# Issuing the first weight load of a decode kernel as 16 partitions and then 112 partitions

## The chip, the cores and the metric

The kernel runs on one core of a Trainium2 chip. The metric is the device time of one execution in microseconds (us), the median of several runs. Beside it stand the profile of one execution (a page of summaries, and views of the trace) and, in the same trace, one record for each packet that the DMA engines moved: its queue, start, length in time and bytes. In the views, PE is the engine of the matrix products, DVE, ACT and POOL are the engines that work on vectors, and SP (SyncE) issues DMAs. The span of a profile is one to two us shorter than the run's time.

## The reference, cut to what matters

One decode step for two tokens. Attention with 16 query heads and 8 key/value heads over a cache of 32,768 positions, a small dense layer beside it, and a gate that mixes the two:

```python
q = (x @ wq)                       # x 2 x 448, wq 448 x 4096
scores = einsum("bhqd,bhkd->bhqk", q, k) * (Dh ** -0.5)
o = einsum("bhqk,bhkd->bhqd", softmax(scores), v)
a = o @ wo
b = gelu(x @ w1 + b1) @ w2 + b2
return g * a + (1 - g) * b
```

The K and V caches are 512 MiB, everything else together about 10 MB. Each byte is read once, so the time is the time to read it (547.43 MB at the 430 GB/s of before's page are 1273 us).

## The kernel before

SBUF holds a ring of three slots of 64 KB per partition. SyncE (SP) issues all large loads in a fixed order: wq and the dense weights share slot 0, then K and V tiles of 8 MB rotate through the slots.

```python
order = [("WQ", 0), ("W12", 0)]
for i in range(NTILES + LAG):
    if i < NTILES: order.append(("K", i))
    if i >= LAG and i - LAG < LASTV: order.append(("V", i - LAG))
# ... cut ...
for d in order:                                   # SP's program
    for pd in before_of[d]:
        E.wait("pe", released(pd))                # the slot is free
    kind, idx = d
    if kind == "WQ":
        parts = [(wq_f, A_wq[0:KC * P, :].rearrange("(p k) n -> p (k n)", p=P), "d_wq0"),
                 (wq_r, A_wq[KC * P:Dm, :].rearrange("p (h n) -> (p h) n", h=2), "d_wq1")]
        for i, (o, src, _) in enumerate(parts):
            dma(lambda e, o=o, src=src: e.dma_start(o, src), "slot0", ("wq", i))
    # ... W12, WO and the last V cut ...
    else:
        src = kv_src(A_k_cache if kind == "K" else A_v_cache, idx)
        dma(lambda e, src=src, d=d: e.dma_start(cut(slot_of[d], 0, SLOT), src),
            f"slot{slot_of[d]}", ("fill", d))
# ... cut: PE's program begins with the products on wq
E.wait("slot0", ("wq", 1))                        # all of wq has landed
```

`wq_f` has 128 partitions (P = 128) with rows of 3 x 4096 bf16 values, 24,576 bytes, one packet each.

## Time and profile before

| | before |
|---|---|
| time, median | 1274.05 us (1273.9 to 1274.08, 3 runs) |
| span of the profile | 1272.2 us |
| DMA | 9 tenths or more in 39 of 40 slices, 430 GB/s |
| PE, DVE busy | 55%, 54% |
| first packet of the large queue, last large packet | 1.765 us, 1268.105 us |

The page of before, slices of the span (each digit or number is one fortieth of it), and the line of the large queue (packets, megabytes, share of the 16 engines' time):

```profile
DMA  9999999999999999999999999999999999999998
GB/s 409 429 433 429 437 441 427 433 427 441 431 437 435 429 431 433 439 431 437 435 429 431 439 433 431 439 433 429 431 441 431 435 437 431 431 433 439 431 423 353
...
q1 hardware_dynamic: 10804, 547.43, 99.6%
```

The DMA engines never run dry between the first slice and the last. The packet records say it more sharply: from the first packet of this queue (1.765 us) to the last large one (1268.105 us), about 16 packets are in flight. The page's chain of waits names DVE and PE for 34% of the span, but while they work to free one slot, the loads of the others keep the engines full.

The start of before: the timeline of SP's issues (start, duration), the page's line of PE's products on wq (busy, mean ns, idle before), and the page's lines of the two wq loads (KB, us from issue to landing):

```profile
0.74 0.88 SPq L370 DMA_DIRECT2D ring<-in_A_wq_dram  x2
1.67 1.83 SPq L376 DMA_DIRECT2D ring<-in_B_w_dram  x3
3.54 0.98 SPq L391 DMA_DIRECT2D ring<-in_A_k_cache_dram  x2
...
L419 PE MATMUL ps_s<-xT,ring 128*128 128x2 bf16 x128 | 3.6, 165 | 8.2 <-DMA ring<-in_A_wq_dram 8.2
...
ring<-in_A_wq_dram SPq DMA_DIRECT2D x1, 3072.0 KB, 10.6
ring<-in_A_wq_dram SPq DMA_DIRECT2D x1, 512.0 KB, 11.4
```

SP is far ahead of the engines: K's first load is issued at 3.54 us and its first packets start at 18.56 us.

The same start by windows (busy time of each engine, the granted clock, the share of the DMA engines, GB/s):

```profile
2.00:10.00 8.00, 0.27 (x5) 0.21 (x5) 2.48 (x11) 1.45 (x2) 1.88 (x5) 1.00 0.87 357
10.00:18.00 8.00, 4.97 (x165) 4.42 (x165) 1.85 (x7) 1.33 (x3) 0.00 (x0) 1.00 1.04 432
...
100.00:1200.00 1100.00, 597.62 (x3768) 114.37 (x1461) 597.04 (x436) 34.86 (x154) 0.00 (x0) 0.78 1.00 433
```

A packet is counted where it starts, so short windows swing a little; the full rate of this kernel is the 433 GB/s of the last line.

### The profile page before, as it was taken

What the parts mean: (1) busy time and instruction counts of PE and PEld (TensorE: products, weight loads), DVE (VectorE), ACT (ScalarE), POOL (GpSimd) and SP (SyncE); (2) the same over time, 40 slices, a digit from 0 to 9 for tenths busy, and PEclk for the clock granted to TensorE, in tenths of its full rate; (3) what the DMA queues carried; (4) which work ended last, traced back from release to release, by engine and by line L of the source; (5) the groups of instructions that cost most, each with busy time, mean ns of one, the idle gap of its engine ahead of it and who ended that gap; (6) DMA issues with size and microseconds to landing.
All of it is one profiled execution on the core that took longest, in us unless ns stands there. A gap on an engine that the chain in (4) does not pass through costs nothing.

```text
span 1272.2 us, 8282 instructions
## 1 busy us (share of the span) xinstructions
PE 693.5 (55%) x4640; PEld 145.3 (11%) x2112; DVE 686.0 (54%) x529; ACT 43.8 (3%) x184; POOL 3.3 (0%) x14
## 2 busy tenths in 40 slices
PE   4566566545566444765445655445664546654465
PEld 3111111100111000111001111001110001110011
DVE  2675546745376553655635567353665536556351
ACT  1000000000000000000000000000000000000000
POOL 1000000000000000000000000000000000000000
PEclk9978887777887677877778877788877788867786
DMA  9999999999999999999999999999999999999998
GB/s 409 429 433 429 437 441 427 433 427 441 431 437 435 429 431 433 439 431 437 435 429 431 439 433 431 439 433 429 431 441 431 435 437 431 431 433 439 431 423 353
DMA packets 10973, 547.62 MB, mean 430 GB/s; under 512 B 1352, under 2 KB 1616, under 8 KB 1872
## 3 DMA queue, kind: packets, MB, share of 16 engines
q1 hardware_dynamic: 10804, 547.43, 99.6%
q8 instruction: 9, 0.15, 0.0%
q14 instruction: 4, 0.03, 0.0%
q10 hardware_dynamic: 156, 0.01, 0.0%
HBM read 547.43 MB, written 0.00 MB: 430 GB/s over the span
## 4 chain that ended last, share of the span: by engine, by line
DMA 63%; DVE 20%; PE 14%; issue 3%; SPq 0%; another core or an unknown queue 0%; DVEq 0%
DMA ring<-in_A_k_cache_dram 60%; DVE ring L720 18%; PE ps_s L487 4%; PE ps_s L334 4%; PE ps_o L334 3%; DMA ring<-in_A_v_cache_dram 3%; DVE mx L724 1%; PE ps_o L536 1%; PE ps_m L496 0%; PE ps_m L501 0%; DVE gmax L726 0%; PE ps_f L548 0%; DVE gmx L730 0%; SPq L376 0%
## 5 line engine op out<-in xcount | busy, mean ns | idle before, releaser
L720 DVE STREAM_TRANSPOSE ring<-ring 128x2048 uint32<-128x2048 uint32 x256 | 565.2, 2274 | 393.0 <-DMA ring<-in_A_k_cache_dram 392.8
L487 PE MATMUL ps_s<-ring,Abd 128*128 128x512 bf16 x1024 | 426.1, 416 | 429.8 <-DVE ring L720 429.4
L334 PE MATMUL ps_s<-ring,Abd 128*128 128x512 bf16 x1024 | 422.8, 413 | 0.0
L487 PEld LDWEIGHTS ps_s<-ring,Abd 128*128 128x128 bf16 x1024 | 106.0, 104 | 851.5 <-DVE ring L720 483.5
L334 PE MATMUL ps_o<-ring,PT 128*24 128x512 bf16 x1504 | 111.9, 404 | 0.0
L536 PE MATMUL ps_o<-ring,PT 128*24 128x512 bf16 x544 | 57.1, 418 | 12.8 <-DMA ring<-in_A_v_cache_dram 12.8
L506 PE MATMUL ps_f<-o_sb,selg 128*32 128x257 f32 x32 | 17.0, 636 | 83.4 <-DVE o_sb L761 83.4
L761 DVE SCALAR_TENSOR_TENSOR o_sb<-ps_o,mask,o_sb 128x256 f32<-128x256 f32 x112 | 54.2, 484 | 9.1 <-PE ps_o L536 5.1
L724 DVE TENSOR_REDUCE mx<-ps_s 128x1 f32<-128x1024 f32 x16 | 19.6, 1225 | 60.0 <-PE ps_s L334 60.0
L632 ACT ACTIVATE negm<-ps_m 128x1 f32<-128x1 f32 x16 | 2.7, 171 | 1157.6 <-PE ps_m L501 1157.6
L737 DVE STREAM_TRANSPOSE PT<-pexp 128x1024 bf16<-128x1024 bf16 x16 | 19.9, 1244 | 36.8 <-PE ps_o L334 36.8
L536 PEld LDWEIGHTS ps_o<-ring,PT 128*24 128x24 bf16 x544 | 14.6, 98 | 102.3 <-issue 85.3
L734 DVE COPY ls<-lsum 128x1 f32<-128x1 f32 x16 | 2.5, 154 | 31.8 <-ACT pexp L636 31.8
L626 ACT COPY Abd<-qrep 32x16 bf16 (+1 forms) x128 | 19.4, 199 | 0.6
L636 ACT ACTIVATE pexp<-ps_s,negm 128x1024 bf16<-128x1024 f32 x16 | 17.8, 1113 | 1.7
L496 PE MATMUL ps_m<-ident_f,mx 128*1 128x128 f32 x32 | 6.1, 270 | 21.1 <-DVE mx L724 21.1
L758 DVE TENSOR_SCALAR o_sb<-ps_o,mask 128x256 f32<-128x256 f32 x16 | 7.6, 475 | 15.7 <-PE ps_o L334 15.7
L506 PEld LDWEIGHTS ps_f<-o_sb,selg 128*32 128x32 f32 x32 | 2.9, 141 | 101.5 <-DVE o_sb L761 101.5
L501 PE MATMUL ps_m<-ones_f,gmx 1*128 1x1 f32 x32 | 6.0, 256 | 9.9 <-DVE gmx L730 9.9
L726 DVE TENSOR_REDUCE gmax<-ps_m 1x2 f32<-1x128 f32 x16 | 4.5, 278 | 7.5 <-PE ps_m L496 7.5
L419 PE MATMUL ps_s<-xT,ring 128*128 128x2 bf16 x128 | 3.6, 165 | 8.2 <-DMA ring<-in_A_wq_dram 8.2
L501 PEld LDWEIGHTS ps_m<-ones_f,gmx 1*128 1x128 f32 x32 | 4.7, 183 | 14.6 <-DVE gmx L730 14.6
(76 smaller groups left out, 61.5 us busy)
## 6 DMA issues: line engine op xcount, KB each, us to landing
ring<-in_A_v_cache_dram SPq DMA_DIRECT2D x1, 4096.0 KB, 26.8
ring<-in_A_v_cache_dram SPq DMA_DIRECT2D x2, 2048.0 KB, 33.5
ring<-in_A_wq_dram SPq DMA_DIRECT2D x1, 3072.0 KB, 10.6
ring<-in_B_w_dram SPq DMA_DIRECT2D x1, 1568.0 KB, 17.9
ring<-in_A_wo_dram SPq DMA_DIRECT2D x1, 1568.0 KB, 32.4
ring<-in_B_w_dram SPq DMA_DIRECT2D x1, 1344.0 KB, 13.7
ring<-in_A_wo_dram SPq DMA_DIRECT2D x1, 1344.0 KB, 35.3
ring<-in_A_wq_dram SPq DMA_DIRECT2D x1, 512.0 KB, 11.4
```

The costliest lines, as they stand in the source:

```text
L334: return e.add_instruction(mybir.InstMatmult(name=f"I-{nc.next_id()}", engine=mybir.EngineType.PE, ldweights=False, ins=[e.lower_ap(x), e. ...
L487: fn = lambda e, o=o, x=x, st=st, sp=sp, s=s, w=w: e.matmul(o, a_win(s, w), x, start=st, stop=sp, skip_group_check=True)
L501: E.ins(lambda e: e.matmul(ps_m[:, C_BC:C_BC + 1], gmx[:, :], ones_f[0:1, 0:1], start=True, stop=True), key=("M2", g))
L506: E.ins(lambda e: e.matmul(ps_oa, selg[:, :], o_sb[:, :], start=False, stop=False, skip_group_check=True), key=("OT", g))
L536: fn = lambda e, o=o, x=x, wt=wt, st=st, sp=sp, j=j: e.matmul(o, wt, x, start=st, stop=sp, skip_group_check=True)
L626: E.ins(lambda e, o=o, Q=Q, c=c: e.copy(o[:, :, c:c + 2], qrep[32 * Q:32 * Q + 32, :, bass.ds(E.dyn(2 * g, 2), 2)]), key=(("A", g) if (Q = ...
L636: E.ins(lambda e: e.activation(pexp[:, :].rearrange("p (r i a) -> p i r a", r=CR, i=2), ps_s[:, :].rearrange("p (i r a) -> p i r a", i=2, ...
L720: E.ins(lambda e: e.transpose(k_words(idx, blk), k_words(idx, blk)), key=("T", idx, blk))
L724: E.ins(lambda e: e.tensor_reduce(mx[:, :], ps_s[:, :], AX.X, ALU.max), key=("MX", g))
L737: E.ins(lambda e: e.transpose(PT[:, :], pexp[:, :]), key=("PT", g))
L758: E.ins(lambda e, p=p, m=m: e.tensor_scalar(o_sb[:, 0:Dh], p, m, None, op0=ALU.mult), key=("OS0", g))
L761: E.ins(lambda e, p=p, m=m: e.scalar_tensor_tensor(out=o_sb[:, 0:Dh], in0=p, scalar=m, in1=o_sb[:, 0:Dh], op0=ALU.mult, op1=ALU.add), key= ...
```

## The change

The likely intent is an earlier first byte: a first DMA with few rows might be ready sooner, with the other 112 rows right behind it. All else stays, and PE still waits for all of wq.

```diff
                 if kind == "WQ":
-                    parts = [(wq_f, A_wq[0:KC * P, :].rearrange("(p k) n -> p (k n)", p=P), "d_wq0"),
-                             (wq_r, A_wq[KC * P:Dm, :].rearrange("p (h n) -> (p h) n", h=2), "d_wq1")]
-                    for i, (o, src, _) in enumerate(parts):
+                    src = A_wq[0:KC * P, :].rearrange("(p k) n -> p (k n)", p=P)
+                    parts = [(wq_f[0:16, :], src[0:16, :]), (wq_f[16:P, :], src[16:P, :]),
+                             (wq_r, A_wq[KC * P:Dm, :].rearrange("p (h n) -> (p h) n", h=2))]
+                    for i, (o, src) in enumerate(parts):
                         dma(lambda e, o=o, src=src: e.dma_start(o, src), "slot0", ("wq", i))
...
-                E.wait("slot0", ("wq", 1))
+                E.wait("slot0", ("wq", 2))
```

## The prediction

> **What bounds the kernel.** Its DMA stream, from almost the first microsecond to the last four. The slices show DMA 9 tenths in 39 of 40, 430 GB/s over the span. The packet records of the big queue (q1) show 16 packets in flight from its first packet, at 1.74 us, to 1268.1 us of a span of 1272.2 us. Compute sits inside that: PE 55%, DVE 54%. The chain of waits names DVE and PE for 34%, but while they free a slot, the loads of other slots keep the queue full. So a microsecond won or lost by the stream at the start should come out, nearly whole, at the end.
>
> **What changes.** The same 3072 KB of wq move in two DMAs (16 rows of 24,576 B, one for each of 16 engines; then 112 rows, seven each) instead of one of 128 (eight each). PE still waits for all of wq.
>
> 1. *One more issue on SP:* 0.41 us (timeline, 0.74 to 1.15). Cost 0: the first packets last until 3.3 us or later, the second DMA is issued by about 1.6 us, and K's first load, issued at 3.54, moves data only at 18.5 us.
> 2. *Perhaps an earlier first byte* (the likely intent). Issue begins at 0.74, first packet at 1.74, the engines start over 0.33 us. I take −0.15 us.
> 3. *Where the rows land.* [...] a packet of 24,576 B takes 0.912 us. [...] Some hides behind the cold start, since the first packets take 1.4 to 2.5 us already: I take +2.2.
> 4. *The 112 rows.* [...] +1.8 us, ±0.5 for unevenness.
>
> No trace of before has a large load on fewer than 128 partitions[...].
>
> **On the critical path:** all of 2, 3 and 4, since the stream has no slack. Sum: −0.15 + 2.2 + 1.8 = about +3.9 us, to 1278.0 us (+0.3%). [...] Range 1273.6 to 1281.5. Faster by over 2% 0.003, within 2% 0.99, slower by over 2% 0.007: even wq at a quarter rate throughout costs about 22 us, under 2%.
>
> **What would show it.** The first 16 packets of q1: right if they take about 3 to 3.7 us, wrong if 1.4 to 2.5. The 112 rows: packets of up to twice 0.912 us. PE's first product on wq (now 12.73 us) and K's first packets (18.54 us) some 3 to 5 us later; steady packets of 65,536 B still 2.42 us; the last packet later by the same; idle times of PE and DVE moved, not grown.
>
> **What would make it wrong.** [...] rows dealt in strides of 16 instead of blocks of seven[...]; engines that fall behind at the start without setting the end; a first byte that gains more than 0.3 us.

The forecast's sum came to −0.15 + 2.2 + 1.8, about +3.9 us, so 1278.0 us. The +2.2 us for the 16 rows (2.7 us for longer packets, less 0.5 for what hides behind the slow first ones) and the +1.8 us for the 112 rows: both were assumed, and no trace of before showed them.

(The prediction's 1.74 and 18.54 us for the first packets of the queue and of K are the 1.765 and 18.56 us of the packet records above.)

## More of the kernel before

The experiments ran in several sets on different chips; the median of before was 1274.03 to 1274.14 us in each set of repeated runs.

The end of before (timeline), which will matter later; the output is issued by SP once ACT and DVE have written it:

```profile
1269.03 0.50 ACT L653 CAST pexp<-ps_f 2x112 bf16<-2x112 f32 x2 [41.61 <-PE ps_f L548]
1269.03 0.54 DVE L792 CAST pexp<-ps_f 2x112 bf16<-2x112 f32 x2 [3.27 <-PE ps_f L548]
1269.96 0.34 SPq L395 DMA_DIRECT2D out_dram<-pexp  x1
```

## The result, and the profile after

The time after is 1279.09 us (1278.34 to 1279.26, 4 runs), before 1274.07 us (4 runs): 5.0 us more. The ratio is 1.0038, 95% interval 1.0021 to 1.0056, so slower, by far less than 2%. (A ratio here is the mean time of one kernel's fast runs over that of the other's of the same rounds, so not quite the ratio of the medians that are quoted.) It was inside the predicted range (1273.6 to 1281.5), with 1278.0 as the forecast.

The page of after, slices and queue:

```profile
DMA  9999999999999999999999999999999999999998
GB/s 315 452 429 426 435 427 442 431 427 437 431 441 429 427 439 431 441 429 427 439 431 441 429 427 439 431 441 429 427 439 433 439 429 427 439 433 439 429 422 368
...
q1 hardware_dynamic: 10820, 547.43, 99.7%
```

The engines are as "busy" as before, with the same bytes, but the first slice moved 315 GB/s in place of 409. So the busy share does not tell the rate: in the windows from 2 to 10 us below and above, shares of 0.86 and 0.87 stand beside 200 and 357 GB/s. The start of after, the same three views (the last line is from the list of all DMA issues, since the page leaves it out):

```profile
0.74 1.38 SPq L371 DMA_DIRECT2D ring<-in_A_wq_dram  x3
2.15 1.46 SPq L377 DMA_DIRECT2D ring<-in_B_w_dram  x3
3.66 0.91 SPq L392 DMA_DIRECT2D ring<-in_A_k_cache_dram  x2
...
L420 PE MATMUL ps_s<-xT,ring 128*128 128x2 bf16 x128 | 3.6, 165 | 14.1 <-DMA ring<-in_A_wq_dram 14.1
...
ring<-in_A_wq_dram SPq DMA_DIRECT2D x1, 2688.0 KB, 16.0
...
ring<-in_A_wq_dram SPq DMA_DIRECT2D x1, 512.0 KB, 16.8
...
ring<-in_A_wq_dram SPq DMA_DIRECT2D x1, 384.0 KB, 5.5
```

The further issue on SP cost nothing: K's first load is issued 0.12 us later, some 20 us before it is due. PE's wait for wq grew from 8.2 to 14.1 us. By windows:

```profile
2.00:10.00 8.00, 0.27 (x5) 0.21 (x5) 2.08 (x10) 1.45 (x2) 1.88 (x5) 1.00 0.86 200
10.00:18.00 8.00, 0.00 (x0) 0.00 (x0) 1.98 (x7) 0.20 (x1) 0.00 (x0) 1.00 0.92 257
...
100.00:1200.00 1100.00, 613.27 (x3791) 116.81 (x1472) 603.20 (x439) 34.90 (x154) 0.00 (x0) 0.77 1.00 433
```

The loss is all in the first 18 us: 200 and 257 GB/s in place of 357 and 432. From 100 us on the rate is 433 in both. The packet records of the 128 rows of `wq_f`, taken sixteen at a time in order of start (so, one packet for each engine, although the records do not name the engine):

```
              before                         after
round   median start  median length    median start  median length   rows of
  0        1.88           1.74            1.86           2.55        the DMA of 16
  1        3.59           0.94            4.42           2.20        the DMA of 112
  2        4.52           0.92            6.62           1.65
  3        5.45           0.91            8.26           1.40
  4        6.37           0.91            9.67           1.29
  5        7.28           0.91           10.98           1.36
  6        8.20           0.91           12.35           1.64
  7        9.11           0.91           13.99           1.51
K's first 18.85           2.42           24.91           2.42
```

The first packet started at 1.755 us against 1.765: nothing was gained there. The median length was longer in all eight rounds, and from round 1 on the shortest packet of after (1.25 us) was longer than the longest of before (0.97 us). K's first packets started 6.1 us later (24.91 less 18.85), and the last large packet of the kernel ended 6.1 us later (1274.20 less 1268.11). Yet the span grew by only 5.1 us. From the last large packet to the end of the span there are 4.08 us before and 3.05 us after. So there is a loss of 6.1 us at the start, and a gain of 1.0 us at the end that nobody had asked for. Here is the end of after; the output's issue follows the writes by less than in before:

```profile
1275.11 0.50 ACT L654 CAST pexp<-ps_f 2x112 bf16<-2x112 f32 x2 [41.82 <-PE ps_f L549]
1275.11 0.54 DVE L793 CAST pexp<-ps_f 2x112 bf16<-2x112 f32 x2 [3.27 <-PE ps_f L549]
1275.71 0.32 SPq L396 DMA_DIRECT2D out_dram<-pexp  x1
```

### The profile page after: what moved, and what is told of

It is laid out like the page before. It is cut to its first block, busy times and chain, and to the rows that moved or that the text cites. A ratio compares the mean times of both kernels' runs of the same rounds, so it can differ in the third digit from the quotient of the medians.

```text
span 1277.3 us, 8288 instructions
## 1 busy us (share of the span) xinstructions
PE 700.7 (55%) x4640; PEld 146.1 (11%) x2112; DVE 685.9 (54%) x529; ACT 43.9 (3%) x184; POOL 3.3 (0%) x14
## 4 chain that ended last, share of the span: by engine, by line
DMA 63%; DVE 18%; PE 16%; issue 3%; SPq 0%; another core or an unknown queue 0%; DVEq 0%
DMA ring<-in_A_k_cache_dram 60%; DVE ring L721 16%; PE ps_s L488 5%; PE ps_s L334 5%; PE ps_o L334 4%; DMA ring<-in_A_v_cache_dram 3%; PE ps_o L537 1%; DVE mx L725 1%; PE ps_m L502 0%; PE ps_m L497 0%; DVE gmax L727 0%; PE ps_f L549 0%; DVE gmx L731 0%; SPq L377 0%
## 5 line engine op out<-in xcount | busy, mean ns | idle before, releaser
L334 PE MATMUL ps_o<-ring,PT 128*24 128x512 bf16 x1504 | 115.8, 416 | 0.0
L537 PE MATMUL ps_o<-ring,PT 128*24 128x512 bf16 x544 | 58.4, 428 | 12.7 <-DMA ring<-in_A_v_cache_dram 12.7
L420 PE MATMUL ps_s<-xT,ring 128*128 128x2 bf16 x128 | 3.6, 165 | 14.1 <-DMA ring<-in_A_wq_dram 14.1
```

The lines of the kernel that those rows point to most:

```text
L334: return e.add_instruction(mybir.InstMatmult(name=f"I-{nc.next_id()}", engine=mybir.EngineType.PE, ldweights=False, ins=[e.lower_ap(x), e. ...
L537: fn = lambda e, o=o, x=x, wt=wt, st=st, sp=sp, j=j: e.matmul(o, wt, x, start=st, stop=sp, skip_group_check=True)
```

## The experiments

The theory: the partitions that the DMA engines write at the same time set the length of the packets, and 16 neighbouring partitions at a time make them longer than the single load of all 128 does. The texts call this the ports theory, after the picture of what lies behind it. No run shows that picture. The packets of 3.65 and of about 1.8 us in the expectations were assumed; measured were 3.17 to 3.29 (blocks16) and 1.75 to 1.92 us (stride8, half64). Rival A: an additional DMA, or a small one, costs the time by itself. Rival C: the small first DMA spoils the cold start, in which packets are slow anyway (a median of 1.74 us in round 0 of before, 0.91 to 0.94 in the later rounds). Later rivals concern the HBM side, and how rows are dealt to engines. The record marks all runs as correct, and that includes blocks16_src8, whose edit permutes rows of wq: so the check does not notice a wrong wq, and its mark says little about the edits. The diffs show the deciding lines only: the load of `wq_r` is kept in all, and PE always waits for the whole of wq.

### cols: the same two sizes, cut by columns

```diff
+ parts = [(wq_f[:, a:b], src[:, a:b]) for a, b in ((0, 1536), (1536, KC * HD))]
```

> wq's first load in two DMAs as in the change, but cut by columns: 128 rows of 3,072 B, then 128 rows of 21,504 B. The byte split is the change's (1/8, 7/8), the count of DMAs is the change's, and every DMA has all 128 partitions. Ports theory: no loss, 1274.1 us within 0.5, K's first packets at 18.6 us. Rival A (a further DMA in the queue, or a small first one, costs the time): about 1279 us, as the change.

1272.97 us (1272.8 to 1273.86) against 1274.03 of before, ratio 0.9993 (0.9976 to 1.0010). The bytes of both DMAs are those of the change, and nothing is lost. PE's wait for wq, from the page of cols:

```profile
L420 PE MATMUL ps_s<-xT,ring 128*128 128x2 bf16 x128 | 3.5, 165 | 7.9 <-DMA ring<-in_A_wq_dram 7.9
```

Rival A falls. The median is even 1 us below before; that was not expected, and is taken up under k0_cols. Since cols has as many DMAs as the change, it is the fairer kernel to compare the change with: 1279.09 less 1272.97 is 6.1 us, the loss that the packets show.

### blocks16, stride8, half64: which partitions are written together

```diff
+ parts = [(wq_f[16 * j:16 * j + 16, :], src[16 * j:16 * j + 16, :]) for j in range(8)]   # blocks16
+ parts = [(wq_f[j:P:8, :], src[j:P:8, :]) for j in range(8)]                             # stride8
+ parts = [(wq_f[a:a + 64, :], src[a:a + 64, :]) for a in (0, 64)]                        # half64
```

> The same load as eight DMAs of 16 neighbouring partitions. Ports theory: [...] packets of 24,576 B take 2.5 us (what the first 16 of the change took) to 3.65 us[...], and the load 20 to 29 us in place of 7.3: 1286 to 1296 us. Rival A (a cost per DMA, 5 us for one more): 35 us more, 1309 us. Rival C (only the cold start suffers): 1279 us or less, packets after the first 16 at 0.91 us.

> Eight DMAs of 16 partitions as in blocks16, but each takes every eighth partition[...]. Ports theory: packets of 24,576 B about 1.8 us, the load some 14.6 us in place of 7.3: about 1281 us, a third of the loss of blocks16. Rivals A and C: the same as blocks16, since number, size and row count of the DMAs are the same.

> Two DMAs of 64 partitions, 0 to 63 and 64 to 127, four rows for each engine. Ports theory with rows dealt in blocks (as I take it for the 112 rows): [...] packets 1.8 us, the load 14.6 us: about 1281 us. Rows dealt in strides of 16: [...] packets 2.5 to 3.65 us, 1286 to 1296 us. Rival A: 1279 us. Rival C: 1279 us or less, packets of the second half 0.91 us.

| | partitions of one DMA | time, us | packets of rounds 1 to 7, medians, us | over cols, us | K's first packets (median) later than in cols, us |
|---|---|---|---|---|---|
| blocks16 | 16 neighbouring | 1291.33 | 3.17 to 3.29 | 18.4 | 18.0 |
| stride8 | 16, 8 apart | 1280.42 | 1.75 to 1.90 | 7.5 | 7.5 |
| half64 | 64 neighbouring | 1280.92 | 1.79 to 1.92 | 8.0 | 7.8 |
| before | all 128 | 1274.03 | 0.91 to 0.94 | | |

(The times over cols are differences of the medians.) PE's wait for wq, from the pages of blocks16, stride8 and half64:

```profile
L420 PE MATMUL ps_s<-xT,ring 128*128 128x2 bf16 x128 | 3.6, 165 | 25.8 <-DMA ring<-in_A_wq_dram 25.8
```
```profile
L420 PE MATMUL ps_s<-xT,ring 128*128 128x2 bf16 x128 | 3.6, 165 | 15.5 <-DMA ring<-in_A_wq_dram 15.5
```
```profile
L420 PE MATMUL ps_s<-xT,ring 128*128 128x2 bf16 x128 | 3.6, 165 | 15.7 <-DMA ring<-in_A_wq_dram 15.7
```

blocks16 and stride8 issue the same number of DMAs, of the same size and row count; only which partitions stand together differs, and the loss is 18.4 against 7.5 us. The choice of partitions makes the difference, and both times are as expected for it (1286 to 1296 us, and about 1281); rivals A and C had the same loss for both, and C fails too because late packets are as slow as early ones (3.17 to 3.29 us in rounds 1 to 7). A round of 16 packets of 24,576 bytes in 3.2 us is 123 GB/s, in 1.75 to 1.92 us 205 to 225; the window from 10 to 20 us shows 121 GB/s in blocks16, that from 5 to 10 us 222 in stride8 and 212 in half64. (In stride8 and half64 the first packet also came 0.3 to 0.4 us later, at 2.13 and 2.08 us against 1.76 in cols, which is a small part of their loss.) half64 also tells something of how rows are dealt to engines. Dealt in strides of 16, each of its rounds would write 16 neighbouring partitions, as blocks16 does, whose packets took 3.17 to 3.29 us; they took 1.79 to 1.92. That fits a deal in blocks of four neighbouring rows. How the single load of 128 rows is dealt, no run tells. And delays at the start reach the end whole: the last two columns agree within 0.4 us.

### blocks16_src8: SBUF's side or HBM's

```diff
+ parts = [(wq_f[16 * j:16 * j + 16, :], src[j:P:8, :]) for j in range(8)]
```

> Wrong result on purpose (rows of wq permuted): the partitions of blocks16, fed from the rows of HBM that stride8 reads together. If the SBUF side limits (ports): blocks16's time, 1291.3 us. If the HBM side does (which rows are read together): stride8's, 1280.4 us.

1290.99 us; packets of rounds 1 to 7 have medians of 3.16 to 3.30 us. It is blocks16's time. The time follows the partitions that are written (blocks16, 1291.33 us), not the rows of HBM that are read (stride8, 1280.42 us).

### swap: the 112 rows first

```diff
+ parts = [(wq_f[0:112, :], src[0:112, :]), (wq_f[112:P, :], src[112:P, :])]
```

> 112 rows (0 to 111) first, then the 16 rows 112 to 127. Ports theory: the same sum in another order, the 16 rows [...] 3.2 us a packet: 1278 to 1280 us. Rival C (a small first DMA spoils the cold start): with 112 rows first the loss goes, 1273 to 1274 us.

1279.58 us (1279.35 to 1279.61). The loss does not need a small DMA at the start: rival C falls. Here the last 16 packets of the load took 2.0 to 3.2 us.

### k0_16_112: the same cut on K's first load

```diff
+ rows = (0, 16, P) if d == ("K", 0) else (0, P)
+ for a, b in zip(rows, rows[1:]):
+     dma(... cut(slot_of[d], 0, SLOT)[a:b, :], src[a:b, :] ...)
```

> wq as before; the first load of K (rows of 65,536 B, running after 18 us) in 16 and 112 partitions. Ports theory: the loss scales with bytes, 6.1 us x 65,536 / 24,576 = 16.3 us over a kernel with the same number of DMAs and no loss (1273.0): about 1289 us; packets of the 16 rows 3.2 x 2.67 = 8.5 us in place of 2.42. Rival C: no loss, 1273 to 1274 us. Rival A: 1279 us.

1295.75 us (1294.4 to 1296.69), 22.8 us over cols. Rivals A and C fall again, but the size is a miss: 16.3 us were expected. The packets say where the other 6.5 us are. The 16 rows took a median of 8.65 us, as expected, 6.2 more than the 2.42 of a full load; but in the change the first round cost only 0.85 us, presumably because part of the added time hid behind the cold start (no run isolates this), and scaled by 2.67 that is 2.3. This is 3.9 us of the miss. The seven rounds of the 112 rows had a mean of 4.46 us (of the medians), where the change's, 1.58 us, scales to 4.21: seven times 0.25 is 1.8. And the first packets of the next K load, which meet the last of the 112 rows, took 3.2 us in place of 2.42: 0.8. So the cut is dearer in the middle of a stream than at its cold start, by more than its bytes.

### stride7: how the 112 rows are dealt

```diff
+ parts = [(wq_f[0:16, :], src[0:16, :])] + [(wq_f[16 + j:P:7, :], src[16 + j:P:7, :]) for j in range(7)]
```

> The change's first DMA of 16 rows, then the other 112 rows as seven DMAs of 16 rows, 7 partitions apart (16, 23, 30 ...; then 17, 24, 31 ...). If the single DMA of 112 rows deals blocks of seven neighbouring rows, these are the very sets of partitions that its rounds write: the change's time again, 1279.1 us within 0.7, and packets of the same lengths (medians 2.2, 1.65, 1.4, 1.3, 1.35, 1.6, 1.5 us). If the 112 rows are dealt otherwise: another time. [...]

1278.89 us, and medians of 2.17, 1.67, 1.44, 1.26, 1.33, 1.63 and 1.58 us for the seven rounds, within 0.07 us of the change's in each. So the single DMA of 112 rows behaves as one that deals blocks of seven neighbouring rows, whose rounds write partitions 7 apart. No packet of any round is near 0.91 us: the shortest of all 112 took 1.16 us. This is where the prediction's picture broke: it let only a few packets of a round be slow, by an estimate whose working is cut. Why the rounds differ among themselves, from 1.26 to 2.17 us, no run tells.

### four_same and four_apart: whose packets become longer

One run each. An extra small DMA of four rows, into partitions 0 to 3 in four_same and 0, 4, 8 and 12 in four_apart, runs just ahead of K's first load; K's load then uses all 128 partitions as always. The question is whether the small DMA slows only the few engines that it concerns (the "sharers" of the text) or the others too. (SP also waits for the small DMA before K's third load; the diff leaves this out.)

```diff
+ xo = cut(0, W_WQ + W_W12, FREE)[0:4:1, :]     # four_same; [0:16:4] in four_apart
+ xi = kv_src(A_k_cache, 0)[0:4:1, 0:FREE]
+ dma(lambda e: e.dma_start(xo, xi), "d_ex", "ex")
```

> before with one extra small DMA ahead of K's first load, into memory that is free then: 4 rows of 11,776 B into partitions 0 to 3, so 4 of the 16 engines[...]. Both theories: the four extra packets about 4 x 0.437 = 1.7 us (11,776 / 24,576 of 0.912 us is 0.437). Only the sharers suffer (as predicted): of K's first 48 packets of 65,536 B, [...] at most a few[...] differ. All suffer: most of K's first 16 packets[...] are longer than 2.5 us.

> The control of four_same: the same four rows into partitions 0, 4, 8 and 12[...]. Extra packets 0.44 us each, K's packets all 2.42 us.

Packet lengths in us:

```
              the four extra packets     K's first 16 packets
four_same     0.44 0.47 0.80 1.49        13 of 3.01 to 3.25, and 2.88, 2.62, 2.47
four_apart    0.44 0.45 0.45 0.45        15 of 2.42 to 2.43, and 2.88
```

(The next 48 packets of both are 2.42 to 2.43 us.) The bytes are the same, the rows of HBM differ a little, and at most four of the 16 engines have an extra packet (taking one packet in flight for each engine, as in before's records, where about 16 are in flight). With the four partitions apart nothing happens (a single packet of 2.88 us stands in both); with the four neighbouring ones, 13 of the first 16 packets of K's load became 0.6 to 0.8 us longer, and at least nine of these ran on engines that had no extra packet. So here four packets to neighbouring partitions held up engines that had no part in them. Why, no run here tells.

### k0_cols and wait_sp: the microsecond at the end

```diff
+ cols = (0, SLOT // 8, SLOT) if d == ("K", 0) else (0, SLOT)     # k0_cols: two DMAs by columns
+ if d == ("K", 0): E.wait("pool", "ts1")                         # wait_sp: one wait more on SP
```

> wq as before, in one DMA; the first load of K in two DMAs of 128 partitions, cut by columns (1/8, 7/8). It asks why cols is 1.06 us faster than before. Tail theory: [...] the fetch of two 8 KB blocks that stands before the output's packets at 1270.6 us of before lies elsewhere: 1273.0 us, and no such fetch between the output's issue and its packets. Rival (cols gains because wq's first packets are short): 1274.0 us, as before.

> before with one more wait in SyncE's program, on a memset-like instruction done at 4.0 us, ahead of K's first load: no transfer is changed. Tail theory, if a few instructions are enough to move the fetch: 1273.0 us; if they are not: 1274.0 us, and the fetch still there. No theory expects more than 0.2 us over before.

k0_cols took 1273.11 us (1272.74 to 1273.48, 5 runs) against 1274.14 (1273.77 to 1274.42, 9 runs) of before; the ranges do not meet, though the interval of the ratio, 0.9978 to 1.0005, includes 1. wait_sp took 1274.12 us. In k0_cols wq is loaded as in before, so cols's gain has nothing to do with wq. The output's issue in k0_cols, then in wait_sp (timelines):

```profile
1269.04 0.54 DVE L794 CAST pexp<-ps_f 2x112 bf16<-2x112 f32 x2 [3.27 <-PE ps_f L550]
1269.65 0.33 SPq L397 DMA_DIRECT2D out_dram<-pexp  x1
```
```profile
1269.13 0.54 DVE L794 CAST pexp<-ps_f 2x112 bf16<-2x112 f32 x2 [3.26 <-PE ps_f L550]
...
1270.07 0.34 SPq L397 DMA_DIRECT2D out_dram<-pexp  x1
```

From the start of DVE's write to the issue it is 0.61 us in k0_cols (0.60 in after), and 0.94 in wait_sp (0.93 in before). The packet records of queue 14, which the profile calls instruction packets, name the difference (start in us):

```
           8 KB instruction packets after 1230 us     the output's two packets
before     1270.60, 1270.65                           1270.71, 1271.07
wait_sp    1270.70, 1270.74                           1270.82, 1271.24
after      1244.15, 1276.71                           1276.46, 1276.49
cols       1237.75, 1270.99                           1270.47, 1270.50
k0_cols    1237.89, 1270.68                           1270.41, 1270.44
```

In before and in wait_sp two of these packets stand between the output's issue and its packets, and the second output packet comes some 0.4 us after the first. In the three others of the list, and in all nine remaining kernels, SP's program has at least one DMA more; there one instruction packet stands 32 to 42 us before the output's packets, and the other after them. The time from the last large packet to the end of the span is 4.1 to 4.2 us in the first two and 3.0 to 3.1 us in all twelve others. So the gain goes with the place of the instruction packets (the "fetch" of the texts), and one wait more on SP (wait_sp) was not enough to move them. Whose instructions they carry, and why a DMA more goes with another place, the trace does not say, and no run moved them alone.

## Why the prediction was right or wrong

**The total and the direction were right:** +3.9 us was forecast and +5.0 measured, within the range and far from 2%. The sum had three terms mis-sized (steps 2 to 4) and one missing.

**Bound by the stream, no slack: right.** Every delay of K's first packets (against cols) arrived at the end within 0.4 us in all of the runs on wq, and the rate from 100 us on stayed at 433 GB/s. The steady packets stayed at 2.42 us, as forecast.

**Step 1, one more issue costs 0: right.** Issuing wq took 1.38 us in place of 0.88, yet K's first load was issued only 0.12 us later, long before it was due. cols has the same number of issues and lost nothing.

**Step 2, an earlier first byte, −0.15 us: wrong, 0.01 us.** The first packet came at 1.755 us with 16 rows and 1.765 with 128. The change's likely aim does not exist here.

**Step 3, the 16 rows, +2.2 us: right that they are slow, too large.** The first packets were forecast at 3 to 3.7 us and took 2.3 to 3.0. By the prediction's own test, right from 3 us and wrong up to 2.5, only one of the 16 is in the first band and six are in the second; it is blocks16 that shows how slow 16 neighbouring rows are, 3.17 to 3.29 us in each of rounds 1 to 7. The next round began 0.83 us later than in before. Two things made it smaller. Sixteen neighbouring rows are faster than assumed: a packet after round 0 took 3.2 us in blocks16, not the assumed 3.65. And more of the added time seems to have hidden behind the cold start than the 0.5 us that I took off, which no run isolates. Some of it may also have been pushed into round 1, which is longer (2.20 us) than the other rounds.

**Step 4, the 112 rows, +1.8 us: right that they are slow, wrong about how many packets are, and so much too small.** Starts from round 1 to K's first packets are 20.5 us apart after and 15.25 before: +5.2 us, part of it perhaps pushed on from round 0. The deal in blocks of seven agrees with stride7. What failed is the estimate of +1.8 us: it slowed only a few packets of a round. four_same shows 13 of 16 packets longer after four small ones, and in every round of the change all 16 packets are long, 1.25 us or more against 0.97 at most before.

**Missing: the end, −1.0 us.** The prediction let the start's loss come out at the end unchanged. It did (6.1 us at the last large packet), but with a DMA more in SP's program, the instruction packets no longer stood just before the output's packets (1270.60 and 1270.65 against 1270.71 us in before; 1276.71 against 1276.46 in after), and 1.0 us less passed from the last large packet to the end (3.05 in place of 4.08). The "+3.9" came near +5.0 partly by luck: the missing gain offset part of a loss that was underrated (3.9 us against 6.1).

## What to carry to other kernels

If a load has to be cut, try columns before partitions: in this DMA-bound kernel, pieces of 128 partitions cost nothing (1272.97 us in cols, 1273.11 in k0_cols, 1274.03 and 1274.14 in before), while each of the eight kernels that cut by partitions lost 5.9 to 22.8 us against cols, and the loss was paid in full at the end. A DMA share of 9 tenths does not show this (the first slice had it at 409 GB/s in before and at 315 in after); look at the GB/s of the stage and at the length of packets of equal size. When two kernels differ by a microsecond, check the last few us for instruction packets before crediting the edit, and use a control with the same number of DMAs.

The experiments point to no change of wq's load that gains. The two cuts by columns (1272.97 and 1273.11 us) have lower medians than both kernels, by 1 us against before, but the gain goes with the moved instruction packets and not with a faster load, and neither interval excludes 1.
